# Two row groups of the TensorE array for h and for the transposes of u, in an attention and feed-forward kernel

## The chip, the cores and the metric

The kernel runs on one core of a Trainium2 chip. The metric is the device time of one execution in microseconds (us). Times of single instructions come from one execution that was recorded with the hardware profiler; they are given in us, or in ns where that is said.

## The reference

Two stages, one behind the other, over 4 batches of 12608 tokens with 128 channels; 49 agents per batch; `d_ff` is 1024. All data is float32.

```python
def sm(a, b):
    s = scale * (a @ b.transpose(0, 2, 1))
    s = s - s.max(-1, keepdims=True)
    e = np.exp(s)
    return e / (e.sum(-1, keepdims=True) + 1e-09)
a2k = sm(agents, k)
agent_v = a2k @ v
q2a = sm(q, agents)
x = (q2a @ agent_v).reshape(B * S, D)

h = x @ w_in
e = np.exp(h - h_max)
solu = h * (e / (e.sum(-1) + 1e-09))
ln = (solu - mu) / np.sqrt(var + 1e-06) * g_ln
out = ln @ w_out
```

## The kernel before, in words

**Tiles.** A tile x is 128 tokens; there are 99 per batch and 396 in all. Everything after the attention is done tile by tile, the softmax of q against the agents in units of 8 tiles and groups of 4, the second matmul w in pairs of tiles, and the output in groups of 4.

**Phase A, once per batch** (`phase_a`): the agents' softmax over the keys and its product with v, in 13 chunks of up to 1024 keys: scores (`p1_mm`, L427), maximum, exp, four transposes (`p2_t`, L460), the product with v (`p2_mm`, L476). Then `agent_v` is multiplied by `w_in` and split into a high and a low fp32r part, `mh` and `ml`, of 1024 columns each (`f3`, `f4h`, `f4l`). The 64 rows of the 49 agents (padded with zeros) stand twice, in partitions 0 to 63 and 64 to 127. Phase A of batch 0 is the head of the kernel; that of each later batch is woven into the tiles of the batch before.

**Phase B, once per 8 tiles** (`phase_b`): scores of q against the agents (`b0`, L657), softmax on DVE and ACT, and for each group of 4 tiles the division into `pack` on POOL (`b4`), two transposes (`b5`, L692), the high part of p on ACT (`b6`, L698), the low part on DVE (`b7`, L703), and DMAs that bring them into `pT` (`b8`, L716).

**Per tile.** h (`c_h`, L757, PE) into one of two PSUM buffers `ph` of two banks each; its maximum (`c_max`, L761, DVE); exp (`c_exp`, L771, ACT); u = h * e / 1024 (`c_u`, L776, DVE); the sum of squares (`c_sq`, L782, ACT); eight 128x128 transposes of u (`c_t`, L789, PE), four to a PSUM bank `px`; each bank copied out (`c_ev`, ACT) either straight into the high part `uH` (L804, then `c_ldir`, L813, subtracts on DVE for the low part `uL`) or into `uT` (L808), from which POOL makes `uH` (`c_sph`, L817) and `uL` (`c_spl`, L821). 5 of 16 banks go the first way. w (`c_w`, L837, PE) is 24 matmuls of 256 columns for a pair of tiles: three products (wH·uH, wH·uL, wL·uH) of eight pieces. The output is scaled with the tokens' factors (`c_rstd`, nine small POOL instructions per four tiles, and `c_fin`, L902, DVE) and stored.

**How h is made of parts.** p = pH + pL stands as 128 rows: 64 of pH and 64 of pL. One matmul of `pT` (128 rows) with `mh` therefore gives (pH + pL)·mh, and a second one with `ml` adds (pH + pL)·ml. With 1024 columns in two halves these are four matmuls of 512 columns per tile.

**Modes of the array.** `p1_mm`, `p2_mm` and `b0` use 64 of the 128 columns each, two at a time, one in each column half (128*64 in the profile); all other matmuls of the kernel before use the whole array (128*128).

**What sets the order.** `Plan` (L26) is a list scheduler that runs when the program is built. Each operation has an engine, a cost, a due time (`at(x, ...)` with the constants `DH` to `DEVL`), dependencies, and may take a PSUM bank (`take`) out of four `px` banks, which another operation gives back (`free`). The plan simulates the engines with its own costs, picks for each engine what can start first, and among those the one due first; the program then has that order on every engine. An operation has a `kind`: 2 for the matmuls in column halves, 0 or 1 for the rest of PE; `SWITCH` is what the plan charges for going from one kind to another, and `HOLD` how much later an operation of the same kind may start and still be preferred. DMAs are all issued by SP, in the plan's order. PE, ACT, DVE, POOL and SP run their own lists in order and wait for each other through semaphores.

Of the kernel before, what the change touches and what calls it, by code (L numbers as in the profile page):

```python
# [25 lines left out]
class Plan:  # L26
# [8 lines left out]
    SWITCH = ((0.0, 0.0, 0.09), (0.0, 0.0, 0.09), (0.15, 0.12, 0.0))  # L35

    HOLD = 0.12
# [28 lines left out]
    def run(self, idle=None):  # L66
        while True:
            best = None
            for e, ops in self.cand.items():
                if not ops:  # L70
                    continue
                free = [b[0] for b in self.banks if b[0] is not None]
                first = min(free) if free else None
                at, opts, low = self.at[e], [], None
                for o in ops:
                    s = max(at, o.ready[e])
                    if o.take:
                        if first is None:
                            continue
                        s = max(s, first)  # L80
# [12 lines left out]
            if best is None:  # L93
                break
            s, e, o = best
            for z in o.eng:
                self.cand[z].remove(o)
            if o.take:
                can = [b for b in self.banks if b[0] is not None and b[0] <= s]
                bank = max(can, key=lambda b: b[0])  # L100
                bank[0], o.bank = None, bank
            if idle is not None and e == "P":
                idle(s - self.at[e])
            o.start, o.by = s, e
            if e == "S":
                hold, size, lag = o.cost
                self.at[e] = s + hold
                if size:
                    self.dma = max(self.dma, s + 2.0) + size / 0.36
                    o.end = self.dma + 0.3  # L110
                else:
                    o.end = s + lag
            else:
                c = o.cost[o.eng.index(e)] if len(o.eng) > 1 else o.cost
                if e == "P":
                    c += self.SWITCH[self.kind][o.kind]
# [16 lines left out]
def kernel(  # L133
# [11 lines left out]
    nc = tc.nc  # L145
# [28 lines left out]
    DMX = 10.86
    DEX = 3.43
    DU_ = -4.09
    DSQ = 18.85
    DT = -0.42
    DEV = 5.18
# [33 lines left out]
    DWL = 1.6  # L213
# [4 lines left out]
    AEND = -1.6  # L218
# [425 lines left out]
    def phase_b(k, dues, gate=()):  # L644
# [50 lines left out]
        def b6(q):  # L695
            w = (min(GT, nt - q * GT) + 1) // 2 * P
            r["n", q] = bpool.tile([P, 2, GT // 2 * P], F32R, tag="pn", bufs=2, name=f"pn{b}_{t0}_{q}")
            nc.scalar.copy(out=r["n", q][:, 0, :w], in_=r["pt", q][:, :w])  # L698
# [35 lines left out]
        for q in range(nq):  # L734
# [5 lines left out]
            B5[k, q] = op("P", lambda px, q=q: b5(q, px), 0.218, dues[5] + 2.5 * q, [B4[k, q]], take=True, shy=shy)  # L740
            a6 = op("A", lambda q=q: b6(q), 0.25, dues[5] + 2.5 * q + 0.3, [B5[k, q], pT_op[groups[g - 2]] if g > 1 else None], shy=shy)
            d7 = op("D", lambda q=q: b7(q), 0.33, dues[5] + 2.5 * q + 0.6, [a6], free=B5[k, q], shy=shy)
            pT_op[groups[g]] = op("S", lambda q=q: b8(q), (0.24, 0.13 if k else 0, 3.0), dues[5] + 2.5 * q + 0.6,
                                  [d7, grp_h.get(groups[g - PTB]) if g >= PTB else None], shy=shy)
# [5 lines left out]
    def c_h(x, hf):  # L750
# [3 lines left out]
        lhs = pTs[b, g][:, j * P : (j + 1) * P]  # L754
        sl = slice(hf * HW, (hf + 1) * HW)
        for m in range(2):
            nc.tensor.matmul(ph[:, sl], lhs, bmats[b]["mh" if m == 0 else "ml"][:, sl], start=(m == 0), stop=(m == 1))  # L757
# [27 lines left out]
    def c_t(x, hf, pt):  # L785
        rr[x, hf] = pt
        for kf in range(4):
            k0 = hf * 4 + kf
            nc.tensor.transpose(pt[:, kf * P : (kf + 1) * P], us[x][0][:, k0 * P : (k0 + 1) * P], ident)  # L789
# [4 lines left out]
    def parts(x, k0, k1):  # L794
# [3 lines left out]
        return [t[:, k0:k1, j * P : (j + 1) * P] for t in pr[i]]  # L798

    def c_ev(x, hf):  # L800
        uH, _ = parts(x, hf * 4, hf * 4 + 4)
        pt = rr[x, hf].rearrange("p (k t) -> p k t", t=P)
        if direct(x, hf):
            nc.scalar.copy(out=uH, in_=pt)  # L804
        else:
            if x not in rr:
                rr[x] = epool.tile([P, NF, P], F32, tag="uT", bufs=UTB, name=f"uT{x}")
            nc.scalar.copy(out=rr[x][:, hf * 4 : hf * 4 + 4, :], in_=pt)  # L808

    def c_ldir(x, hf):  # L810
        uH, uL = parts(x, hf * 4, hf * 4 + 4)
        pt = rr[x, hf].rearrange("p (k t) -> p k t", t=P)
        nc.vector.tensor_tensor(out=uL, in0=pt, in1=uH.bitcast(F32), op=ALU.subtract)  # L813

    def c_sph(x, k0, k1):
        uH, _ = parts(x, k0, k1)
        nc.gpsimd.tensor_scalar(out=uH, in0=rr[x][:, k0:k1, :], scalar1=1.0, scalar2=0.0, op0=ALU.mult, op1=ALU.add)  # L817

    def c_spl(x, k0, k1):
        uH, uL = parts(x, k0, k1)  # L820
        nc.gpsimd.tensor_tensor(out=uL, in0=rr[x][:, k0:k1, :], in1=uH.bitcast(F32), op=ALU.subtract)  # L821
# [136 lines left out]
    for x in range(n):  # L958
# [11 lines left out]
        grp_h[b, t // GT] = last_h[b] = H[x, 1]  # L970
        MX[x] = op("D", F(c_max, x), 1.13, at(x, DMX, DMXR, DMXL), [H[x, 0], H[x, 1]])
# [5 lines left out]
        if len(dh) < 2:  # L977
# [3 lines left out]
            if len(utl) <= UTB:  # L981
                buf += wready if (len(utl) + 2) % UTB == 2 else cout
        for hf in range(2):
            T[x, hf] = op("P", F(c_t, x, hf), 0.435, at(x, DT, DTR, DTL) + 0.02 * hf, [U[x]] + buf, take=True)
            EV[x, hf] = op("A", F(c_ev, x, hf), 0.477, at(x, DEV, DEVR, DEVL) + 0.02 * hf, [T[x, hf]],
                           free=None if hf in dh else T[x, hf])
            if hf in dh:
                LD[x, hf] = op("D", F(c_ldir, x, hf), 0.602, at(x, DLD, DLDR, DLDL), [EV[x, hf]], free=T[x, hf])
        need = [[LD.get((x, hf)), EV[x, hf]] for hf in range(2)]
        if len(dh) < 2:  # L990
            k0, k1 = (4 if 0 in dh else 0), (4 if 1 in dh else NF)
            SH[x] = op("G", F(c_sph, x, k0, k1), 0.17 + 0.107 * (k1 - k0), at(x, DSP, DSPR, DSPL),
                       [EV[x, hf] for hf in range(2) if hf not in dh])
            SP[x] = op("G", F(c_spl, x, k0, k1), 0.16 + 0.268 * (k1 - k0), at(x, DSP, DSPR, DSPL) + 0.02, [SH[x]])
# [6 lines left out]
        if x % 2 == 1:  # L1001
            prev = None
            for m0 in range(0, WM, WC):
# [4 lines left out]
                       need_prev[0] + (need_prev[1] if m1 > WM // 2 else []) + wready + [prev, W.get((i - 1, 1)), FIN.get(G - 2)], take=lead, kind=0)  # L1008
# [79 lines left out]
```

## Time and profile before

| | |
|---|---|
| median of 3 runs | 1539.29 us (1538.47 to 1539.41) |
| profiled execution | 1537.99 us, span 1535.9 us |
| granted TensorE clock | 0.998 |
| matmuls | 12643 |
| DMA | 159.65 MB, mean 104 GB/s |

The span runs from the first to the last instruction of the profiled execution. In the views, `out<-in` are the tiles that an instruction writes and reads; `xN` counts instructions; the mean duration of one is in ns. In the groups of instructions the last field is the idle time of the engine before them and what ended it. In the list of waits stand the waiting engine with its instruction, what it waited for, the total in us, how often, and the longest. PE is TensorE's matmuls, PEld its weight loads, DVE VectorE, ACT ScalarE, POOL GpSimd, SP the engine that issues DMAs. A float32 matmul that isn't a transpose is recorded as two.

### The profile page before, as it was taken

The page shows a single profiled execution, that of the slowest core. Times are in us where ns is not written, and L with a number is a line of the kernel's source. Part 1 is how long each engine was busy: PE and PEld are TensorE (multiplying, and loading weights), DVE is VectorE, ACT ScalarE, POOL GpSimd, SP SyncE. Part 2 cuts the span into 40 slices and gives each one's busy share as a digit, 9 for nine tenths or more (in the row PEclk, how much of TensorE's full clock was granted, in tenths as well). Part 3 has the DMA queues.
Part 4 walks back from the last instruction along what each step waited for, and adds up shares of the span by engine and source line. Part 5 has one row for each costly group of instructions (what it writes and reads, how often), then busy time and mean ns, then how long its engine had stood idle before and what let it go on. Part 6 is the DMA issues. An engine that isn't in the chain of part 4 may idle for free.

```text
span 1535.9 us, 35549 instructions
## 1 busy us (share of the span) xinstructions
PE 1509.6 (98%) x12643; PEld 1352.4 (88%) x12643; DVE 1366.4 (89%) x2201; ACT 1424.4 (93%) x2747; POOL 1251.6 (81%) x1613
## 2 busy tenths in 40 slices
PE   8899999999999999999999999999999999999998
PEld 5688898898888898989898998989998999999988
DVE  7788998898989988988999988889999989999896
ACT  4699999999999999899999999999999999999997
POOL 2469878888887888778877798888888898998987
PEclk9999999999999999999999999999999999999999
DMA  9632423332324332423234332433222323231211
GB/s 371 190 128 73 146 91 111 96 101 94 95 77 151 111 111 90 139 82 104 82 97 136 106 118 87 128 99 104 68 89 61 87 66 90 72 86 56 63 56 46
DMA packets 114720, 159.65 MB, mean 104 GB/s; under 512 B 16240, under 2 KB 71152, under 8 KB 114544
## 3 DMA queue, kind: packets, MB, share of 16 engines
q1 hardware_dynamic: 114544, 157.39, 33.0%
q8 instruction: 100, 1.64, 0.4%
q14 instruction: 76, 0.62, 0.1%
HBM read 105.36 MB, written 26.02 MB: 86 GB/s over the span
## 4 chain that ended last, share of the span: by engine, by line
PE 73%; ACT 9%; POOL 7%; DVE 5%; issue 4%; DMA 2%; DVEq 0%; SPq 0%; ACTq 0%; POOLq 0%
PE px L837 28%; PE ph L757 18%; PE px L789 17%; ACT e L771 4%; POOL uL L821 3%; PE px L476 2%; PE px L427 2%; PE px L657 2%; ACT sq L782 2%; POOL uH L817 2%; ACT uT L808 2%; DVE u L776 1%; PE px L460 1%; PE px L692 1%; POOL y L856 1%
## 5 line engine op out<-in xcount | busy, mean ns | idle before, releaser
L821 POOL TENSOR_TENSOR uL<-uT,uH 128x1024 fp32r<-128x1024 f32 (+1 forms) x344 | 661.9, 1924 | 25.3
L761 DVE TENSOR_REDUCE nm<-ph 128x1 f32<-128x1024 f32 x396 | 479.2, 1215 | 73.9 <-PE ph L757 72.5
L776 DVE SCALAR_TENSOR_TENSOR u<-ph,e 128x1024 f32<-128x1024 f32 x396 | 480.4, 1218 | 41.9 <-ACT e L771 31.1
L782 ACT ACTIVATE sq<-u,su 128x1024 bf16<-128x1024 f32 x396 | 463.7, 1171 | 23.0 <-DVE u L776 19.7
L771 ACT ACTIVATE e<-ph,nm 128x1024 f32<-128x1024 f32 x396 | 449.0, 1137 | 16.9 <-DVE nm L761 15.3
L837 PE MATMUL px<-uL,wH 128*128 128x256 f32 x1584 | 461.6, 291 | 1.3 <-POOL uL L821 1.3
L837 PE MATMUL px<-uH,wH 128*128 128x256 f32 x1584 | 451.9, 285 | 4.2 <-DVE uL L813 2.0
L837 PE MATMUL px<-uH,wL 128*128 128x256 f32 x1584 | 448.8, 283 | 0.0
L789 PE MATMUL px<-ident,u 128*128 128x128 f32 x3168 | 430.1, 273 | 2.8 <-DVE u L776 1.6
L789 PEld LDWEIGHTS px<-ident,u 128*128 128x128 f32 x3168 | 365.2, 141 | 40.1 <-DVE ob L902 2.5
L757 PE MATMUL ph<-mh,pT 128*128 128x512 f32 x792 | 334.3, 422 | 5.2 <-DMA pT<-pn 2.4
L817 POOL TENSOR_SCALAR uH<-uT 128x1024 fp32r<-128x1024 f32 (+1 forms) x344 | 298.5, 868 | 46.8 <-ACT uT L808 44.7
L837 PEld LDWEIGHTS px<-uH,wH 128*128 128x128 f32 x1584 | 298.8, 189 | 19.4 <-issue 5.7
L808 ACT COPY uT<-px 128x512 f32<-128x512 f32 x541 | 301.6, 592 | 13.0 <-PE px L789 4.8
L757 PE MATMUL ph<-ml,pT 128*128 128x512 f32 x792 | 313.0, 395 | 0.1
L837 PEld LDWEIGHTS px<-uL,wH 128*128 128x128 f32 x1584 | 298.9, 189 | 7.9 <-issue 3.0
L837 PEld LDWEIGHTS px<-uH,wL 128*128 128x128 f32 x1584 | 299.0, 189 | 5.5 <-issue 1.4
L813 DVE TENSOR_TENSOR uL<-px,uH 128x512 fp32r<-128x512 f32 x251 | 167.9, 683 | 9.9 <-ACT uH L804 9.2
L757 PEld LDWEIGHTS ph<-mh,pT 128*128 128x128 f32 x792 | 149.6, 189 | 30.6 <-issue 6.8
L757 PEld LDWEIGHTS ph<-ml,pT 128*128 128x128 f32 x792 | 150.2, 190 | 16.5 <-DVE ml L552 0.6
L804 ACT CAST uH<-px 128x512 fp32r<-128x512 f32 x251 | 147.2, 606 | 2.4 <-PE px L789 2.0
L856 POOL TENSOR_TENSOR y<-x,nhalf 128x4 f32<-128x4 f32 x99 | 100.1, 1011 | 7.7
(118 smaller groups left out, 1344.8 us busy)
## 6 DMA issues: line engine op xcount, KB each, us to landing
pT<-pn SPq DMA_DIRECT2D x392, 64.0 KB
rB<-dr SPq DMA_DIRECT2D x98, 256.0 KB
qt<-in_qT_dram SPq DMA_DIRECT2D x48, 512.0 KB
out_dram<-ob SPq DMA_DIRECT2D x95, 256.0 KB
kt<-in_kT_dram SPq DMA_DIRECT2D x36, 512.0 KB
vt<-in_v_dram SPq DMA_DIRECT2D x36, 512.0 KB
dr<-yr SPq DMA_DIRECT2D x392, 0.5 KB
kh<-in_kT_dram SPq DMA_DIRECT2D x12, 512.0 KB
```

The source lines that it names most:

```text
L757: nc.tensor.matmul(ph[:, sl], lhs, bmats[b]["mh" if m == 0 else "ml"][:, sl], start=(m == 0), stop=(m == 1))
L761: nc.vector.tensor_reduce(out=nms[x], in_=phs[x], op=ALU.max, axis=AX.X, negate=True)
L771: nc.scalar.activation(out=es[x], in_=phs[x], func=AF.Exp, bias=nms.pop(x), accum_out=st[G]["S"][:, j : j + 1])
L776: nc.vector.scalar_tensor_tensor(out=u, in0=phs[x], scalar=INV, in1=es[x], op0=ALU.mult, op1=ALU.mult, accum_out=su)
L782: nc.scalar.activation(out=sq, in_=u, func=AF.Square, bias=su, scale=-float(DF), accum_out=st[G]["Q"][:, j : j + 1])
L789: nc.tensor.transpose(pt[:, kf * P : (kf + 1) * P], us[x][0][:, k0 * P : (k0 + 1) * P], ident)
L804: nc.scalar.copy(out=uH, in_=pt)
L808: nc.scalar.copy(out=rr[x][:, hf * 4 : hf * 4 + 4, :], in_=pt)
L813: nc.vector.tensor_tensor(out=uL, in0=pt, in1=uH.bitcast(F32), op=ALU.subtract)
L817: nc.gpsimd.tensor_scalar(out=uH, in0=rr[x][:, k0:k1, :], scalar1=1.0, scalar2=0.0, op0=ALU.mult, op1=ALU.add)
L821: nc.gpsimd.tensor_tensor(out=uL, in0=rr[x][:, k0:k1, :], in1=uH.bitcast(F32), op=ALU.subtract)
L837: nc.tensor.matmul(po, wt[:, kf, :], ut[:, kf, :], start=(q == 0), stop=(q == WM - 1))
```

## The change

- **h** is three products instead of two of doubled rows: pH·mh, pH·ml and pL·mh (pL·ml is left out). Each has 64 rows. The columns 0 to 511 are computed by rows 0 to 63 of the array, 512 to 1023 by rows 64 to 127, into the two banks of `ph`; the two matmuls of a pair follow one another. Six matmuls per tile instead of four.
- **p** is no longer stacked. `pT` has two planes: plane 0 is what ACT and DVE write (high and low part, each with the even tiles of the group in rows 0 to 63 and the odd ones in 64 to 127), plane 1 the same with the row halves exchanged, brought by two DMAs per group instead of four. There are four such tiles instead of eight of half the size.
- **The transposes of u** take 64 tokens each: sixteen instead of eight per tile, with 128 columns of weights and 64 moving columns, the tokens 0 to 63 in rows 0 to 63 and the others in rows 64 to 127, alternating. The two token halves go to two banks, which are both taken when the transposes start (`take=2`).
- **The copies** of a tile's transposes therefore divide by tokens instead of by pieces of `d_ff`: 8 rows of 64 instead of 4 rows of 128 per bank; the same holds for POOL's and DVE's half tiles. Every w matmul now needs both halves.
- **The plan** has a kind 3 for both, which `SWITCH` charges for going in and out, `HOLD` is 0.49 instead of 0.12 and holds for kind 3 too, and the due times are other numbers. Which 5 of 16 banks go straight to `uH` stays.

```diff
-    SWITCH = ((0.0, 0.0, 0.09), (0.0, 0.0, 0.09), (0.15, 0.12, 0.0))
-    HOLD = 0.12
+    SWITCH = ((0.0, 0.0, 0.09, 0.15), (0.0, 0.0, 0.09, 0.15), (0.15, 0.12, 0.0, 0.15), (0.19, 0.19, 0.15, 0.03))
+    HOLD = 0.49
...
-                if e == "P" and self.kind == 2:
-                    near = [z for z in opts if z[0] <= low + self.HOLD and z[1].kind == 2] or near
+                if e == "P" and self.kind >= 2:
+                    near = [z for z in opts if z[0] <= low + self.HOLD and z[1].kind == self.kind] or near
...
-    DH = -3.24
+    DH = -5.61
...
-    PTB = 8
+    PTB = 4
...
-            r["n", q] = bpool.tile([P, 2, GT // 2 * P], F32R, tag="pn", bufs=2, name=f"pn{b}_{t0}_{q}")
-            nc.scalar.copy(out=r["n", q][:, 0, :w], in_=r["pt", q][:, :w])
+            pT = pTs[b, t0 // GT + q] = bpool.tile([P, 2, 2, GT // 2 * P], F32R, tag="pT", bufs=PTB, name=f"pT{b}_{t0}_{q}")
+            nc.scalar.copy(out=pT[:, 0, 0, :w], in_=r["pt", q][:, :w])
...
             for i in range(2):
-                w = (m + 1 - i) // 2
-                r0 = i * AP2
-                for part in range(2):
-                    r1 = r0 if part == 0 else AP2 - r0
-                    nc.sync.dma_start(out=to[r1 : r1 + AP2, :w, i, :].bitcast(F32),
-                                      in_=pn[r0 : r0 + AP2, part, : w * P].rearrange("a (g p) -> a g p", p=P).bitcast(F32))
+                r0, r1 = i * AP2, (1 - i) * AP2
+                nc.sync.dma_start(out=pT[r1 : r1 + AP2, 1, :, :w].bitcast(F32), in_=pT[r0 : r0 + AP2, 0, :, :w].bitcast(F32))
...
-    def c_h(x, hf):
+    def c_h(x):
...
-        sl = slice(hf * HW, (hf + 1) * HW)
-        for m in range(2):
-            nc.tensor.matmul(ph[:, sl], lhs, bmats[b]["mh" if m == 0 else "ml"][:, sl], start=(m == 0), stop=(m == 1))
+        mh, ml = (bmats[b][m] for m in ("mh", "ml"))
+        tok = slice(j // 2 * P, j // 2 * P + P)
+        for q, (part, mm) in enumerate(((0, mh), (0, ml), (1, mh))):
+            for hf in range(2):
+                sl, rows = slice(hf * HW, (hf + 1) * HW), slice(hf * AP2, (hf + 1) * AP2)
+                nc.tensor.matmul(ph[:, sl], pTs[b, g][rows, (hf + j) % 2, part, tok], mm[rows, sl], start=(q == 0), stop=(q == 2))
...
-    def c_t(x, hf, pt):
-        rr[x, hf] = pt
-        for kf in range(4):
-            k0 = hf * 4 + kf
-            nc.tensor.transpose(pt[:, kf * P : (kf + 1) * P], us[x][0][:, k0 * P : (k0 + 1) * P], ident)
+    def c_t(x, *pts):
+        u = us[x][0]
+        for th in range(2):
+            rr[x, th] = pts[th]
+        for k in range(NF):
+            for th in range(2):
+                rows = slice(th * AP2, (th + 1) * AP2)
+                nc.tensor.transpose(pts[th][:, k * AP2 : (k + 1) * AP2], u[rows, k * P : (k + 1) * P], ident[rows, rows])
...
-        for hf in range(2):
-            H[x, hf] = op("P", F(c_h, x, hf), 0.468, at(x, DH, DHR, DHL) + 0.02 * hf,
-                          [pT_op[b, t // GT], U.get(x - 2)] + mdone[b][: hf + 1], kind=0)
+        H[x] = op("P", F(c_h, x), 0.70, at(x, DH, DHR, DHL), [pT_op[b, t // GT], U.get(x - 2)] + mdone[b], kind=3)
...
+        T[x, 0] = T[x, 1] = op("P", F(c_t, x), TCOST, at(x, DT, DTR, DTL), [U[x]] + buf, take=2, kind=3)
         for hf in range(2):
-            T[x, hf] = op("P", F(c_t, x, hf), 0.435, at(x, DT, DTR, DTL) + 0.02 * hf, [U[x]] + buf, take=True)
```

The changed kernel's lines stand one or two away from those before: h is L755, the transposes L790, w L839, the copies into `uT` L810 and into `uH` L806, the DMAs of `pT` L713.

On SP, in the third batch, the DMAs of one group's `pT` and of the scale factors (`dr`, `rB`) before:

```order
L716 DMA pT_96_0_11398<-pn_96_0_11371 64x2x128
L716 DMA pT_96_0_11398<-pn_96_0_11371 64x128
L716 DMA pT_96_0_11398<-pn_96_0_11371 64x2x128
L716 DMA pT_96_0_11398<-pn_96_0_11371 64x128
L878 DMA dr_11438<-yr_11431 4x32 x4
L918 DMA out_dram<-ob_11465 128x512
L879 DMA rB_11439<-dr_11438 128x512
```

and after:

```order
L880 DMA dr_12982<-yr_12974 4x32 x4
L713 DMA pT_96_0_13006<-pT_96_0_13006 64x512 x2
L881 DMA rB_12983<-dr_12982 128x512
L920 DMA out_dram<-ob_13129 128x512
```

The group's DMAs are two, and stand between the write and the broadcast of the scale factors. The places on PE are shown in the prediction.

More of the change, by code (lines that the diff above doesn't have):

```diff
@@ L71, in run @@
                     continue
-                free = [b[0] for b in self.banks if b[0] is not None]
-                first = min(free) if free else None
+                free = sorted(b[0] for b in self.banks if b[0] is not None)
                 at, opts, low = self.at[e], [], None
@@ L77, in run @@
                     if o.take:
-                        if first is None:
+                        if len(free) < o.take:
                             continue
-                        s = max(s, first)
+                        s = max(s, free[o.take - 1])
                     opts.append((s, o))
@@ L99, in run @@
                 can = [b for b in self.banks if b[0] is not None and b[0] <= s]
-                bank = max(can, key=lambda b: b[0])
-                bank[0], o.bank = None, bank
+                o.bank = sorted(can, key=lambda b: -b[0])[: int(o.take)]
+                for b in o.bank:
+                    b[0] = None
             if idle is not None and e == "P":
@@ L119, in run @@
             if o.free is not None:
-                o.free.bank[0] = o.end + self.LAT[e + "P"]
+                of, i = o.free if isinstance(o.free, tuple) else (o.free, 0)
+                of.bank[i][0] = o.end + self.LAT[e + "P"]
             if o.fn:
-                args = [o.bank[1]] if o.take else []
+                args = [b[1] for b in o.bank] if o.take else []
                 if len(o.eng) > 1:
@@ L163 @@
     UB = 8
+    TCOST = 0.496
     TD = 2
     WC = 4
-    BD0 = 11.76
-    BD1 = 15.6
+    BD0 = 13.83
+    BD1 = 17.06
     BD2 = 30.39
-    BD3 = -27.34
-    BD4 = -2.08
-    BD5 = 4.61
-    DH = -3.24
[L174 to L179, printed above, removed]
+    BD3 = -28.93
+    BD4 = -7.3
+    BD5 = 5.96
+    DH = -5.61
+    DMX = 14.19
+    DEX = 1.81
+    DU_ = 16.45
+    DSQ = 23.46
+    DT = -3.69
+    DEV = 3.44
     DLD = 0.41
-    DSP = 17.32
-    DW = 3.32
+    DSP = 16.59
+    DW = 3.39
     DR = 14.7
-    DF_ = 14.05
+    DF_ = 14.12
     OUTD = -4.87
@@ L191 @@
     VLAG = 5.87
-    PTB = 8
+    PTB = 4
     SHY = -0.0
     DHR = -4.39
-    DHL = -5.43
-    DMXR = 17.18
+    DHL = -6.08
+    DMXR = 8.74
     DMXL = 5.41
     DEXR = 23.76
-    DEXL = -1.81
+    DEXL = -4.24
     DUR = -10.07
@@ L204 @@
     DTR = -6.53
-    DTL = -23.89
-    DEVR = -14.39
+    DTL = -24.6
+    DEVR = -8.6
     DEVL = 9.51
     DLDR = -16.1
-    DLDL = 26.96
+    DLDL = 21.86
     DSPR = -6.87
@@ L739, in phase_b @@
             B4[k, q] = op("G", lambda q=q: b4(q), 0.08 + 0.53 * sc, dues[4] + 2.5 * q, [d5, old])
[L740 to L741 removed]
+            B5[k, q] = op("P", lambda px, q=q: b5(q, px), 0.218, dues[5] + 2.5 * q,
+                          [B4[k, q], grp_h.get(groups[g - PTB]) if g >= PTB else None], take=True, shy=shy)
+            a6 = op("A", lambda q=q: b6(q), 0.25, dues[5] + 2.5 * q + 0.3, [B5[k, q]], shy=shy)
             d7 = op("D", lambda q=q: b7(q), 0.33, dues[5] + 2.5 * q + 0.6, [a6], free=B5[k, q], shy=shy)
[L743 to L744 removed]
+            pT_op[groups[g]] = op("S", lambda q=q: b8(q), (0.12, 0.13 if k else 0, 2.5), dues[5] + 2.5 * q + 0.6, [d7], shy=shy)
         if k + 2 < nu and k + 2 > 1:
@@ L797, in parts, with c_ev @@
             pr[i] = [gpool.tile([P, NF, 2 * P], F32R, tag=t, name=f"{t}{x}") for t in ("uH", "uL")]
[L798 to L803, printed above, removed]
+        o = j * P + t0 * AP2
+        return [t[:, :, o : o + (t1 - t0) * AP2] for t in pr[i]]
+    def c_ev(x, th):
+        uH, _ = parts(x, th, th + 1)
+        pt = rr[x, th].rearrange("p (k t) -> p k t", t=AP2)
+        if direct(x, th):
             nc.scalar.copy(out=uH, in_=pt)
@@ L807, in c_ev, with c_ldir, c_sph, c_spl @@
                 rr[x] = epool.tile([P, NF, P], F32, tag="uT", bufs=UTB, name=f"uT{x}")
[L808 to L812, printed above, removed]
+            nc.scalar.copy(out=rr[x][:, :, th * AP2 : (th + 1) * AP2], in_=pt)
+    def c_ldir(x, th):
+        uH, uL = parts(x, th, th + 1)
+        pt = rr[x, th].rearrange("p (k t) -> p k t", t=AP2)
         nc.vector.tensor_tensor(out=uL, in0=pt, in1=uH.bitcast(F32), op=ALU.subtract)
[L815 to L821, printed above, removed]
+    def c_sph(x, t0, t1):
+        uH, _ = parts(x, t0, t1)
+        nc.gpsimd.tensor_scalar(out=uH, in0=rr[x][:, :, t0 * AP2 : t1 * AP2], scalar1=1.0, scalar2=0.0, op0=ALU.mult, op1=ALU.add)
+    def c_spl(x, t0, t1):
+        uH, uL = parts(x, t0, t1)
+        nc.gpsimd.tensor_tensor(out=uL, in0=rr[x][:, :, t0 * AP2 : t1 * AP2], in1=uH.bitcast(F32), op=ALU.subtract)
     WM = 3 * NF
@@ L1007 @@
                 o = op("P", f, 0.1192 * (m1 - m0), at(x, DW, DWR, DWL) + 2.0 * m0 / WM,
-                       need_prev[0] + (need_prev[1] if m1 > WM // 2 else []) + wready + [prev, W.get((i - 1, 1)), FIN.get(G - 2)], take=lead, kind=0)
+                       need_prev[0] + need_prev[1] + wready + [prev, W.get((i - 1, 1)), FIN.get(G - 2)], take=lead, kind=0)
                 if lead:
```

32 lines of the change are left out of this document (15 added, 17 removed).

## The prediction

> **What bounds the kernel now.** I read the page first: its span and the busy time of each engine.
>
> ```profile
> span 1535.9 us, 35549 instructions
> PE 1509.6 (98%) x12643; PEld 1352.4 (88%) x12643; DVE 1366.4 (89%) x2201; ACT 1424.4 (93%) x2747; POOL 1251.6 (81%) x1613
> ```
>
> PE is the fullest, but ACT is close, and a share of the span mixes stages. So next I read the busy times by stretch; the cuts are at the head (before the first h) and about where each batch of 99 tiles ends.
>
> ```profile
> 60.00:435.00 375.00, 365.49 (x3046) 327.09 (x3045) 335.32 (x535) 351.76 (x675) 300.15 (x385) 1.00 0.33 103
> 435.00:809.00 374.00, 370.46 (x3132) 335.12 (x3131) 337.56 (x544) 353.88 (x684) 310.06 (x399) 1.00 0.34 105
> 809.00:1182.00 373.00, 372.69 (x3153) 338.46 (x3151) 335.71 (x539) 355.01 (x688) 310.20 (x401) 1.00 0.33 100
> 1182.00:1519.00 337.00, 334.38 (x2728) 305.99 (x2728) 307.59 (x473) 330.53 (x623) 303.15 (x386) 1.00 0.25 71
> sum 1476.00, PE 1454.98 PEld 1317.50 DVE 1323.91 ACT 1396.96 POOL 1230.56; mean PE 291.00 PEld 263.50 DVE 264.78 ACT 279.39 POOL 246.11
> ```
>
> The columns after the length are PE, PEld, DVE, ACT, POOL. The first three batches, which carry the next batch's phase A, take 374 us each with PE busy nearly all of it; the fourth has no phase A and takes 337 us, and there PE (334) and ACT (331) are both full. The sum runs to the end: PE is busy 1455 of 1476 us after the head, 98.6%. The list of waits agrees: the longest waits of the others are for PE, or for each other; none of PE's own comes near them.
>
> ```profile
> DVE nm L761 <- PE ph L757: 72.5, 117, 2.4
> PE ph L757 <- DMA pT<-pn: 2.4, 2, 1.5
> ```
>
> **The change part by part, on PE.** What h, the transposes and w cost is the distance between starts in the timeline (the second column is a duration, which overlaps the next one).
>
> ```profile
> 800.81 0.40 PE L757 MATMUL ph<-mh,pT 128*128 128x512 f32 x1
> 801.74 0.28 PE L837 MATMUL px<-uH,wL 128*128 128x256 f32 x1
> ...
> 808.41 1.03 PE L789 MATMUL px<-ident,u 128*128 128x128 f32 x8
> 809.20 0.36 PE L837 MATMUL px<-uH,wL 128*128 128x256 f32 x1
> 809.40 0.28 PE L837 MATMUL px<-uH,wH 128*128 128x256 f32 x1
> ```
>
> Four h matmuls lie between 800.81 and 801.74: 0.93 us, 0.235 each. Eight transposes and one w matmul lie between 808.41 and 809.40; a w matmul comes every 0.12 us (366.01 to 366.13 below), so the transposes take 0.87, 0.109 each.
>
> The trace has no matmul in row groups. Its nearest are the matmuls in column groups, L476 and L657, which stand in pairs too:
>
> ```profile
> 366.01 0.28 PE L837 MATMUL px<-uL,wH 128*128 128x256 f32 x1
> 366.13 0.28 PE L837 MATMUL px<-uH,wL 128*128 128x256 f32 x1
> 366.34 1.09 PE L476 MATMUL px<-vt,eT 128*64 128x128 f32 x16
> 367.36 0.38 PE L837 MATMUL px<-uH,wH 128*128 128x256 f32 x1
> 367.58 0.28 PE L837 MATMUL px<-uL,wH 128*128 128x256 f32 x1
> ...
> 399.61 0.40 PE L757 MATMUL ph<-ml,pT 128*128 128x512 f32 x1
> 399.94 2.07 PE L657 MATMUL px<-ag_sb,qt 128*64 128x49 f32 x64
> 401.94 0.33 PE L789 MATMUL px<-ident,u 128*128 128x128 f32 x1
> ```
>
> Three things are read here. First, pairs overlap: 64 matmuls of L657 take 2.00 us, 0.031 each, and 16 of L476 about 0.055 each, half of the 0.109 of a full-array matmul that streams the same 128 f32 columns. Second, changing the array's mode costs: from 366.13 to 367.58 are 1.45 us, less two w (0.24) and 8 pairs of L476 at 0.109 (0.87), so 0.34 for going in and out, 0.17 a change. Third, a first weight load that nothing hides shows in the duration: 0.38 against 0.28 for w (0.10), and 0.33 against the 0.27 of the mean below for a transpose (0.06).
>
> ```profile
> L789 PE MATMUL px<-ident,u 128*128 128x128 f32 x3168 | 430.1, 273 | 2.8 <-DVE u L776 1.6
> ```
>
> h becomes three pairs of 512 columns. If a pair runs as one, 3 x 0.24 = 0.72; saved 0.22 a tile, 87 us in 396. Ends: 0.235 a pair (two at once) and 0.47 (one after the other); I take 0.24, because the column pairs do overlap.
>
> The transposes become eight pairs of 64 moving columns, each member with a load of 128 columns. Half of 0.109 is 0.054, L657's pair takes 0.058 with loads of 64 columns (2.00 less 0.14 of the mode change, over 32), and the load by itself is 0.06. I take 0.06: 8 x 0.06 = 0.48; saved 0.39, 154 us. Ends: 0.054 and today's 0.109.
>
> The mode changes are counted in PE's order: 154 before, 879 after, since nearly every tile has its own block of row-group work (393 blocks). 725 more at 0.175 (0.17, and the load that opens a block is a transpose's 0.06 or an h's 0.10 where L476's was about 0.05) are +127 us. Ends: 0.09 (66 us) and 0.20 (145 us).
>
> PE's sum: 1455 - 87 - 154 + 127 = **1341 us**, 114 less.
>
> **What is next: ACT.** The change gives ACT no work to save. Its time per tile, from start to start:
>
> ```profile
> 815.70 1.15 ACT L782 ACTIVATE sq<-u,su 128x1024 bf16<-128x1024 f32 x1 [0.23 <-DVE u L776]
> ...
> 816.85 1.05 ACT L808 COPY uT<-px 128x512 f32<-128x512 f32 x2
> 817.79 1.12 ACT L771 ACTIVATE e<-ph,nm 128x1024 f32<-128x1024 f32 x1
> ...
> 818.89 0.59 ACT L808 COPY uT<-px 128x512 f32<-128x512 f32 x1
> 819.35 0.61 ACT L804 CAST uH<-px 128x512 fp32r<-128x512 f32 x1
> ```
>
> sq 1.15, two copies 0.94, exp 1.10: 3.19 a tile, 1263 us in 396. The small groups add about 85 after the head:
>
> ```profile
> L698 ACT CAST pn<-px 128x256 fp32r<-128x256 f32 x100 | 38.7, 387 | 2.1 <-PE px L692 2.0
> L453 ACT ACTIVATE ek<-px,nmp 128x512 f32<-128x512 f32 x48 | 33.0, 688 | 15.9 <-DVE nmp L439 15.5 <-PE ph L757 0.2
> L673 ACT ACTIVATE logits<-logits 128x392 f32<-128x392 f32 x48 | 25.3, 529 | 7.8 <-DVE logits L669 7.3
> L466 ACT COPY eT<-px 128x512 f32<-128x512 f32 x34 | 20.3, 596 | 8.4 <-PE px L460 8.4
> L444 ACT ACTIVATE fc<-nmp 128x1 f32<-128x1 f32 x48 | 14.2, 297 | 0.0
> ```
>
> (131.5 in all; a quarter of the 67.5 of L453, L466 and L444 lies in the head; and a row overlaps the next by about 0.13, as the copy of 0.59 above that is followed after 0.46, which is 32 us in some 245 instructions: 83.) So ACT is occupied for about 1350 us after the head: far below PE's 1455 today, but above PE's 1341 afterwards. ACT ends last, by little. Its copies now write rows of 64 (128x8x64) instead of 128. L673, in rows of 49, takes 529 ns where the line from 256 columns (387) to 512 (596) gives 498: 0 to 0.03 a copy, 0 to 24 us. I take 0; rows of 128 into uH cost no more than the contiguous ones (the copies stand about 0.47 apart either way).
>
> POOL keeps its instructions with rows of 64; busy 1231, and 303 of 337 in the fourth batch, so below ACT unless it is slower by a tenth. DVE, 1324 busy, keeps its own.
>
> **What moves in the order.** PE, in the third batch, around one tile (px are the four free PSUM banks, ph the two h buffers, pack the source of pT), before:
>
> ```order
> L837 MATMUL px_126<-uH_10191,wH 128x256
> L692 MATMUL px_124<-ident,pack_110 128x128 x2
> L757 MATMUL ph_123<-mh_5767,pT_72_1_10228 128x512
> L757 MATMUL ph_123<-ml_5768,pT_72_1_10228 128x512
> L757 MATMUL ph_123<-mh_5767,pT_72_1_10228 128x512
> L757 MATMUL ph_123<-ml_5768,pT_72_1_10228 128x512
> L789 MATMUL px_127<-ident,u_10429 128x128 x4
> L789 MATMUL px_125<-ident,u_10429 128x128 x4
> L837 MATMUL px_126<-uL_10192,wH 128x256
> ```
>
> and after, the end of one block of row-group work:
>
> ```order
> L790 MATMUL px_126<-ident,u_12506 128x64
> L790 MATMUL px_124<-ident,u_12506 128x64
> L755 MATMUL ph_123<-mh_6444,pT_80_1_12023 128x512 x2
> L755 MATMUL ph_123<-ml_6445,pT_80_1_12023 128x512 x2
> L755 MATMUL ph_123<-mh_6444,pT_80_1_12023 128x512 x2
> L839 MATMUL px_127<-uL_12343,wH 128x256
> ```
>
> One transpose of a tile and one h, in either order, share a block, so a tile pays for one way in and one way out. A transpose now needs both its banks free before it starts: PE stands behind the later of two copies where it stood behind one, and w is queued behind it.
>
> On SP a group's pT was four DMAs and is two, of the same bytes in all; PE's waits for them were 2.4 us, so I cost it at nothing. pT's first half is now written by ACT and DVE directly, into one of four buffers instead of eight, so ACT's write waits for the DMA and the h of four groups (16 tiles) ago, long done; without that distance it would stop ACT's queue.
>
> **The sum.** The head stays, 60 us. After it two engines have 1341 and 1350 us of work. PE alone at the limit kept 98.6%; in the fourth batch, the nearest case of two full engines, ACT's 3.19 a tile and 0.11 for L698 and L673 (64.0, less 148 x 0.13, over 396) are over 98 tiles 323 of 337 us, 96%. 1350 / 0.96 = 1406; 60 + 1406 = 1466 span. The profiled execution took 1537.99 for a span of 1535.9, 2.1 more, and lies 1.3 under the median 1539.29: **1469 us**, 4.6% less.
>
> **The rivals.**
>
> *Loads pace the transposes (slower).* If a load of 128 columns in a row group takes as long as one of w, 0.10 to 0.11, each pair waits for its loads, at 0.109: the transposes save nothing, PE has 1455 - 87 + 127 = 1495, /0.986 = 1516, 1579 us. It decides from 0.096 a pair, where 8 x (0.109 - 0.096) x 396 = 40 no longer pays the 127 less the 87. Against it: a transpose's load that nothing hides showed 0.06. The Trainium skill, "TensorE: Matmul & The Clock Gate", section "LDWEIGHTS (loading the stationary operand)", gives columns / 1.2 ns however few rows are loaded, an estimate of 107 ns for each of these; w's 0.10 agrees with it, the transposes' 0.06 doesn't. 0.08.
>
> *Pairs overlap only in part.* A pair of h that takes a third longer than one matmul (0.31, a third of the way from 0.235 to 0.47) costs 3 x 0.07 x 396 = 83 more, PE 1424, /0.986 = 1444, 1507 us: faster still, but PE remains the bound. L476's pairs, at twice 0.055, show no such loss, which speaks against it. The Trainium skill, "TensorE: Matmul & The Clock Gate", section "Part 3: Packing small matmuls", gives 3.07 times for four row groups; by that ratio, as an estimate, 0.235 / 0.77 = 0.31. With this case goes PE held up by the two banks: 0.1 us a tile is 40 us, 1509. 0.17.
>
> *Row groups don't run side by side at all.* h 6 x 0.235 = 1.41, +186 us; transposes 16 x 0.06, +36; changes +127: 1804 / 0.986 = 1830, 1893 us. 0.03.
>
> *Both engines run as full as PE did.* 1350 / 0.986 = 1369, 1433 us. 0.07.
>
> **How the numbers follow.** The forecast has 0.65. The range goes from the last rival, 1433, to past the second with the copies' bound of 0.03 (12 of 24 us), 1520; outside are the two slower cases, 0.11, and about half of the 0.07 and of the tail above: 0.17. About 0.2%, 3 us, is what a measurement of this kernel can tell from no change. Faster 0.87; slower 0.11; between the two, 0.02, if a pair lands at 0.096.
>
> **What would show it.** Right: L755 pairs 0.24 apart, eight L790 pairs in 0.48, 0.17 a mode change, PE busy about 1340 to 1400, ACT above 96% of each batch. Wrong: pairs at 0.11 or h at 0.47; ACT's copies above 0.5 start to start; PE waiting for ACT's copies (banks) by more than 40 us; the fourth batch not under 337 us.

## The result, and the profile after

| | before | after |
|---|---|---|
| median | 1539.35 us | 1514.11 us |
| ratio | | 0.9838, 95% interval 0.9821 to 0.9855 |
| span of the profiled execution | 1535.9 us | 1512.5 us |

The changed kernel is 1.6% faster. The forecast was 1469 us, 4.6%: the direction is right, the size is off by a factor of nearly three. One execution of the experiment with h alone took 2990.62 us where its three others took 1594.92 to 1597.61, and its median below is that of the three.

The page's line of busy times, after:

```profile
PE 1438.1 (95%) x16609; PEld 1169.1 (77%) x16609; DVE 1369.3 (91%) x2211; ACT 1408.6 (93%) x2737; POOL 1253.6 (83%) x1613
```

PE isn't full any more, and no other engine is. PE's busy time counts a duration that overlaps the next one, so what was saved is better read from starts. The timeline of PE, one block of row-group work in the third batch:

```profile
804.45 0.71 PE L790 MATMUL px<-ident,u 64*128 64x64 f32 x16
804.97 0.48 PE L755 MATMUL ph<-mh,pT 64*128 64x512 f32 x2
805.28 0.39 PE L755 MATMUL ph<-ml,pT 64*128 64x512 f32 x2
805.52 0.40 PE L755 MATMUL ph<-mh,pT 64*128 64x512 f32 x2
805.84 0.39 PE L839 MATMUL px<-uH,wH 128*128 128x256 f32 x1
806.06 0.31 PE L839 MATMUL px<-uL,wH 128*128 128x256 f32 x1
```

Sixteen transposes take 0.52 us, of which about 0.06 is the first load: 0.06 a pair. The first pair of h takes 0.31, as the first h matmul behind transposes did before (803.47 to 803.78); the second and third stand 0.24 apart. From the third pair at 805.52 to w at 805.84 are 0.32, 0.24 for the pair and 0.08 to 0.09 for the change of mode, and w's second matmul comes 0.22 later instead of 0.12, the load of 0.10 that nothing hides. Each PE term of the sum came out near its forecast.

The stretches of the batches after, cut at the first maximum of each (the columns are length, PE, PEld, DVE, ACT, POOL):

```profile
62.00:423.00 361.00, 344.73 (x4056) 280.86 (x4054) 332.73 (x539) 344.30 (x669) 299.22 (x383) 0.99 0.35 107
423.00:785.00 362.00, 349.65 (x4079) 285.82 (x4077) 334.87 (x541) 349.46 (x681) 307.49 (x395) 1.00 0.36 109
785.00:1155.00 370.00, 357.11 (x4200) 292.16 (x4196) 340.24 (x552) 351.32 (x684) 312.32 (x401) 1.00 0.34 103
1155.00:1489.00 334.00, 313.94 (x3650) 261.36 (x3649) 306.77 (x469) 327.39 (x622) 304.26 (x391) 0.99 0.24 70
1489.00:1512.50 23.50, 15.63 (x136) 13.55 (x134) 10.56 (x15) 8.12 (x16) 8.48 (x13) 0.84 0.09 29
```

By the same mark (first maxima at 60.1, 433.0, 808.8 and 1178.9 us, the last at 1519.1) the batches before took 373, 376, 370 and 340 us. So the first two gained 12 and 14 us, the third nothing, and the fourth, which had two full engines already, 6. The end after the last maximum is 23.5 us, 6.5 longer than the 17 before. Most of PE's saving didn't arrive in the time. The list of waits shows where it went; first before:

```profile
POOL x L853 <- ACT sq L782: 73.6, 68, 4.3
...
POOL uH L817 <- ACT uT L808: 44.7, 33, 10.4
DVE u L776 <- ACT e L771: 31.1, 88, 1.3
...
PEld px L837 <- issue: 10.1, 23, 0.8
...
PEld px L837 <- POOL uL L821: 3.3, 6, 1.5
...
PEld ph L757 <- DVE u L776: 2.4, 5, 0.8
```

and after:

```profile
POOL x L855 <- ACT sq L780: 72.4, 48, 6.5
PEld px L839 <- issue: 48.7, 132, 0.8
DVE u L774 <- ACT e L769: 41.0, 89, 2.0
PEld ph L755 <- DVE u L774: 36.2, 81, 1.0
POOL uH L819 <- ACT uT L810: 31.7, 24, 8.7
DVE nm L759 <- PE ph L755: 29.8, 57, 2.5
PEld px L839 <- POOL uL L823: 18.8, 28, 3.4
```

DVE's wait for h fell from 72.5 to 29.8, and POOL's waits for ACT, which were there before, fell a little. What grew is DVE's wait for ACT (31.1 to 41.0) and, above all, the waits of PE's weight loads: for DVE to read h out of its buffer (2.4 to 36.2), for POOL (3.3 to 18.8), and for nothing that the profile shows (10.1 to 48.7, for the loads of w). The chain that ended last, as shares of the span, says the same; first before:

```profile
PE 73%; ACT 9%; POOL 7%; DVE 5%; issue 4%; DMA 2%; DVEq 0%; SPq 0%; ACTq 0%; POOLq 0%
```

and after:

```profile
PE 41%; ACT 25%; DVE 21%; issue 9%; POOL 3%; DMA 1%; ACTq 0%; DVEq 0%; SPq 0%; POOLq 0%
```

Before, one engine carried the end; after, the chain runs through three.

### The profile page after: what moved, and what is told of

It is laid out like the page before. It is cut to its first block, busy times and chain, and to the rows that moved or that the text cites. A ratio compares the mean times of both kernels' runs of the same rounds, so it can differ in the third digit from the quotient of the medians.

```text
span 1512.5 us, 43191 instructions
## 1 busy us (share of the span) xinstructions
PE 1438.1 (95%) x16609; PEld 1169.1 (77%) x16609; DVE 1369.3 (91%) x2211; ACT 1408.6 (93%) x2737; POOL 1253.6 (83%) x1613
## 4 chain that ended last, share of the span: by engine, by line
PE 41%; ACT 25%; DVE 21%; issue 9%; POOL 3%; DMA 1%; ACTq 0%; DVEq 0%; SPq 0%; POOLq 0%
PE px L839 18%; PE ph L755 9%; ACT e L769 8%; ACT sq L780 7%; PE px L790 6%; DVE u L774 6%; ACT uT L810 6%; DVE nm L759 6%; DVE uL L815 3%; PE px L478 2%; ACT uH L806 2%; PE px L429 2%; POOL uL L823 2%; PE px L659 1%; DVE ob L904 1%
## 5 line engine op out<-in xcount | busy, mean ns | idle before, releaser
L759 DVE TENSOR_REDUCE nm<-ph 128x1 f32<-128x1024 f32 x396 | 477.2, 1214 | 30.8 <-PE ph L755 29.8
L780 ACT ACTIVATE sq<-u,su 128x1024 bf16<-128x1024 f32 x396 | 470.9, 1189 | 16.5 <-DVE u L774 14.4
L839 PE MATMUL px<-uH,wH 128*128 128x256 f32 x1584 | 463.5, 293 | 14.9 <-ACT uT L810 9.3
L839 PE MATMUL px<-uL,wH 128*128 128x256 f32 x1584 | 454.4, 287 | 8.6 <-POOL uL L823 8.4
L839 PE MATMUL px<-uH,wL 128*128 128x256 f32 x1584 | 455.6, 288 | 0.0
L755 PE MATMUL ph<-mh,pT 64*128 64x512 f32 x1584 | 350.0, 441 | 15.7 <-DVE u L774 13.1
L839 PEld LDWEIGHTS px<-uH,wH 128*128 128x128 f32 x1584 | 299.4, 189 | 52.6 <-issue 23.9
L839 PEld LDWEIGHTS px<-uL,wH 128*128 128x128 f32 x1584 | 299.3, 189 | 29.2 <-issue 13.5
L810 ACT COPY uT<-px 128x512 f32<-128x512 f32 x541 | 308.2, 614 | 13.3 <-issue 6.7
L839 PEld LDWEIGHTS px<-uH,wL 128*128 128x128 f32 x1584 | 299.1, 189 | 16.2 <-issue 11.4
L790 PEld LDWEIGHTS px<-ident,u 64*128 64x128 f32 x6336 | 240.5, 139 | 78.3 <-ACT uT L810 14.0
L790 PE MATMUL px<-ident,u 64*128 64x64 f32 x6336 | 272.4, 226 | 12.0 <-DVE uL L815 3.1
L755 PEld LDWEIGHTS ph<-mh,pT 64*128 64x128 f32 x1584 | 150.7, 186 | 88.7 <-DVE u L774 36.2
L755 PE MATMUL ph<-ml,pT 64*128 64x512 f32 x792 | 158.4, 394 | 0.1
L806 ACT CAST uH<-px 128x512 fp32r<-128x512 f32 x251 | 151.8, 625 | 1.8 <-PE px L790 1.8
L769 ACT ACTIVATION_READ_ACCUMULATOR e<-ph,nm 128x1 f32 x396 | 93.2, 235 | 0.0
```

Source lines behind the costliest of these rows:

```text
L755: nc.tensor.matmul(ph[:, sl], pTs[b, g][rows, (hf + j) % 2, part, tok], mm[rows, sl], start=(q == 0), stop=(q == 2))
L759: nc.vector.tensor_reduce(out=nms[x], in_=phs[x], op=ALU.max, axis=AX.X, negate=True)
L769: nc.scalar.activation(out=es[x], in_=phs[x], func=AF.Exp, bias=nms.pop(x), accum_out=st[G]["S"][:, j : j + 1])
L780: nc.scalar.activation(out=sq, in_=u, func=AF.Square, bias=su, scale=-float(DF), accum_out=st[G]["Q"][:, j : j + 1])
L790: nc.tensor.transpose(pts[th][:, k * AP2 : (k + 1) * AP2], u[rows, k * P : (k + 1) * P], ident[rows, rows])
L810: nc.scalar.copy(out=rr[x][:, :, th * AP2 : (th + 1) * AP2], in_=pt)
```

## The experiments

The question was what holds the time now: PE still (theory P), ACT (A), POOL (Q), the ring of h, maximum, exp and u through the two h buffers (R), waits that the row groups bring (B), or no engine alone, because four lists in a fixed order wait for each other in turn (S). Each run's median stands beside the kernel before on the same chip (medians of 1539.8 to 1540.6 us in the four sets, so a comparison across sets is good to about a microsecond) or beside the changed kernel's 1514.

### Half of sq: less for ACT, outside the ring

```diff
-        nc.scalar.activation(out=sq, in_=u, func=AF.Square, bias=su, scale=-float(DF),
+        nc.scalar.activation(out=sq[:, :HW], in_=u[:, :HW], func=AF.Square, bias=su, scale=-float(DF),
```

> The changed kernel with its order kept; the sum of squares reads 512 of the 1024 columns (half of it is left out), so ACT has about 0.43 us a tile less, 170 us in all; sq lies outside the ring h, maximum, exp, u, next h. If ACT alone is the bound (theory A): 1450 to 1475, where PE's 1341 us of work take over at 96%. If the ring through the two h buffers with its queueing is the bound (theory R): 1495 or more, at most 20 off. If PE is still the bound through mode changes and its own waits (theory P): 1508 to 1520.

Measured: 1484.98 us, ratio to before 0.9645 (0.9621 to 0.9668), 29 less than the changed kernel. None of the three bands: ACT matters more than R and P say, but of 170 us taken out of it 29 arrive.

### Half of exp: less for ACT, inside the ring

```diff
-        nc.scalar.activation(out=es[x], in_=phs[x], func=AF.Exp, bias=nms.pop(x), accum_out=st[G]["S"][:, j : j + 1])
+        nc.scalar.activation(out=es[x][:, :HW], in_=phs[x][:, :HW], func=AF.Exp, bias=nms.pop(x), accum_out=st[G]["S"][:, j : j + 1])
...
-        nc.vector.scalar_tensor_tensor(out=u, in0=phs[x], scalar=INV, in1=es[x], op0=ALU.mult, op1=ALU.mult, accum_out=su)
+        nc.vector.scalar_tensor_tensor(out=u.rearrange("p (h f) -> p h f", h=2), in0=phs[x].rearrange("p (h f) -> p h f", h=2), scalar=INV,
+                                       in1=es[x][:, :HW].unsqueeze(1).to_broadcast([P, 2, HW]), op0=ALU.mult, op1=ALU.mult, accum_out=su)
```

> The changed kernel with its order kept; exp is computed for 512 of the 1024 columns and u uses those twice (half of exp is left out). ACT is relieved by the same 170 us as with the halved sq, but inside the ring. A: the same as with the halved sq, 1450 to 1475. R: clearly less than with the halved sq, by 25 or more, 1440 to 1465. P: 1508 to 1520.

Measured: 1482.97, 0.9627 (0.9606 to 0.9648). The same as with the halved sq within 2 us, as A says, though not in A's band. That the cut lies in the ring makes no difference: R falls.

### One of w's three products left out: less for PE

```diff
-            mm += [(wH, uH, kf), (wH, uL, kf), (wL, uH, kf)]
+            mm += [(wH, uH, kf), (wH, uL, kf), None]
```

> The changed kernel with its order kept; w leaves out the product of uH with the low part of w, 16 matmuls a pair of tiles instead of 24: PE has 187 us less. P: 1430 to 1460, ACT's 1350 at 96 to 98%. A: 1500 to 1515. R: 1495 to 1515, since w is outside the ring and delays it only where an h is queued behind it.

Measured: 1504.51, 0.9764 (0.9743 to 0.9784); 10 less for 187 us of PE's work. P falls; the time lies in the bands of A and of R. The waits of this run show what takes PE's place:

```profile
PEld ph L755 <- DVE u L774: 109.0, 191, 1.9
...
PE ph L755 <- DVE u L774: 62.1, 129, 1.7
```

PE, done early, stands before h until u has left the buffer: its wait for DVE rises from 36 and 13 us to 109 and 62.

### Half of the maximum: less for DVE

```diff
-        nc.vector.tensor_reduce(out=nms[x], in_=phs[x], op=ALU.max, axis=AX.X, negate=True)
+        nc.vector.tensor_reduce(out=nms[x], in_=phs[x][:, :HW], op=ALU.max, axis=AX.X, negate=True)
```

> The changed kernel with its order kept; the maximum reads 512 of the 1024 columns (half of it is left out): DVE has about 0.5 us a tile less, inside the ring. R: 1450 to 1480. A and P: 1505 to 1518, as DVE is neither's bound.

Measured: 1501.32, 0.9747 (0.9727 to 0.9767); 13 less for about 200 us. Below the band of A and P, and far above that of R. DVE now waits 116.6 us for exp where it waited 41.0:

```profile
DVE u L774 <- ACT e L769: 116.6, 167, 2.5
```

### Half of POOL's subtraction

```diff
-        nc.gpsimd.tensor_tensor(out=uL, in0=rr[x][:, :, t0 * AP2 : t1 * AP2], in1=uH.bitcast(F32), op=ALU.subtract)
+        nc.gpsimd.tensor_tensor(out=uL[:, :4], in0=rr[x][:, :4, t0 * AP2 : t1 * AP2], in1=uH[:, :4].bitcast(F32), op=ALU.subtract)
...
-            mm += [(wH, uH, kf), (wH, uL, kf), (wL, uH, kf)]
+            mm += [(wH, uH, kf), (wH, uL, kf % 4), (wL, uH, kf)]
```

> The changed kernel with its order kept; POOL makes the low part of u for four of the eight pieces only, and w uses those twice (half of that subtraction is left out). POOL has about 1.1 us less for a whole tile and 0.6 for a half, some 300 us of its 1330 (start to start, 3.36 a tile). If POOL, counted start to start, is the hidden bound (theory Q): 1430 to 1470. If no engine alone holds the time and the lists wait for each other in turn (theory S): 1485 to 1508, as the three others gave 10 to 31 us each.

Measured: 1509.23, 0.9808 (0.9792 to 0.9825); 5 less, though POOL's busy time fell by 298, and one above S's band:

```profile
PE 1431.7 (95%) x16609; PEld 1166.2 (77%) x16609; DVE 1365.8 (91%) x2211; ACT 1407.7 (93%) x2737; POOL 955.4 (63%) x1613
```

Q falls: POOL's lateness in the trace comes from what it waits for.

### All four cuts at once

The edits for sq, the maximum, w and POOL together (w with `(wH, uL, kf % 4)` and without the third product).

> The changed kernel with its order kept and four cuts at once: half of sq (ACT, 170 us), half of the maximum (DVE, 200 us), one of three products of w (PE, 187 us), half of POOL's subtraction (300 us); each left out as in the single runs. S: the engines wait for each other's full lists, so all cuts together give far more than the sum of the single ones (83 us with POOL's taken as 30): 1300 to 1380. If the ring h, maximum, exp, u through the two h buffers holds the time by its latency (theory R; only the maximum in it is cut, 0.5 us a tile or 0.25 in a ring of two tiles): 1400 to 1440, little more than the sum.

Measured: 1366.99, 0.8881 (0.8867 to 0.8895); 147 less than the changed kernel, where the four singly gave 29 + 13 + 10 + 5 = 57. That is what S says: what one list gains is lost at the next as long as that one stays full. A bound that passes from engine to engine would say it too. And again no engine is full:

```profile
PE 1266.3 (93%) x15025; PEld 984.8 (72%) x15025; DVE 1164.1 (85%) x2211; ACT 1242.2 (91%) x2737; POOL 953.1 (70%) x1613
```

### HOLD at 0.12 and at 0.9

```diff
-    HOLD = 0.49
+    HOLD = 0.12
```

> The changed kernel with HOLD at 0.12 as before: PE's order has 1054 changes of mode instead of 879, 175 more at 0.175, 31 us of work for PE. Theory P (PE's mode changes hold the time): 1540 to 1550. S: the waits take part of it, 1518 to 1540. If the long HOLD costs PE waiting for work of the same mode (theory H): 1490 to 1510.

Measured: 1546.02, 1.0041 (1.0018 to 1.0065); 32 more, as P said and beyond S's band, and for 175 more changes of mode 0.18 us each. Taken alone that fits the price of a change.

```diff
-    HOLD = 0.49
+    HOLD = 0.9
```

> The changed kernel with HOLD at 0.9: 764 changes of mode instead of 879, 20 us less work for PE, and PE may be kept up to 0.9 us for work of the same mode. If each change of mode is paid in full, as the step from 0.12 to 0.49 suggested (175 changes, 32 us): 1490 to 1498. If waiting for work of the same mode takes it back: 1508 to 1535.

Measured: 1545.73, 1.0037 (1.0025 to 1.0049). With 115 changes fewer the kernel is 32 slower as well, beyond both bands. So the agreement of the run before is no proof of P: both numbers give another order, and both other orders cost the same.

### The changed kernel with the due times of before

```diff
-    DH = -5.61
+    DH = -3.24
...
-    DU_ = 16.45
+    DU_ = -4.09
```

(and the other due times of the diff; `HOLD` and `PTB` stay).

> The changed kernel with the due times of the kernel before (HOLD stays 0.49; 896 changes of mode, 17 more, 3 us): the same work on every engine in another order. If the order holds the time (theory S): 1530 to 1600. If the engines' work or their latencies hold it whatever the order: 1512 to 1522.

Measured: 1541.83, 1.0016 (1.0006 to 1.0026). The same work on every engine but for 17 changes of mode more, and all of the gain is gone. With these due times the row groups are worth nothing.

### Each part alone

With the due times of before: h alone (the hunks of `c_h`, `b6` to `b8`, `PTB` and `Plan`), then the transposes alone (`c_t`, `parts`, the copies and `Plan`).

```diff
-        for hf in range(2):
-            H[x, hf] = op("P", F(c_h, x, hf), 0.468, ...
+        H[x] = op("P", F(c_h, x), 0.70, ..., kind=3)
```

> The kernel before with h alone in row groups (p unsplit, its new DMAs and buffers, HOLD 0.49), the transposes as before, the due times as before; to be set beside the run with both parts and the same due times (1541.8). PE's order has 806 changes of mode, 652 more than before: 114 us at 0.175, against 87 saved: 27 more for PE. If the change of mode is paid by either part alone (theory M): 1560 to 1580. If h alone is worth its 87 and the transposes bring only waits: 1490 to 1520.

Measured: 1595.06, 1.0365 (1.0344 to 1.0385); 55 more than before. Most of that is work of PE, which is as full as in the kernel before and 45 us longer busy:

```profile
PE 1554.6 (98%) x13444; PEld 1285.0 (81%) x13444; DVE 1372.8 (86%) x2201; ACT 1428.7 (90%) x2747; POOL 1253.3 (79%) x1613
```

```diff
+        T[x, 0] = T[x, 1] = op("P", F(c_t, x), TCOST, at(x, DT, DTR, DTL), [U[x]] + buf, take=2, kind=3)
         for hf in range(2):
-            T[x, hf] = op("P", F(c_t, x, hf), 0.435, ..., take=True)
```

> The kernel before with the transposes alone in row groups (two banks at once, copies by tokens, HOLD 0.49), h and p as before, the due times as before. 900 changes of mode, 746 more: 131 us, against 147 saved (eight pairs at 0.0625 for 0.87): 16 less for PE. M: 1525 to 1550. If the transposes' need of two banks at once costs by itself (theory B): 1555 or more.

Measured: 1591.35, 1.0332 (1.0316 to 1.0347). Alone each part is over 3% slower, both together 0.2% with the same due times. A tile pays for about one way into row groups and one out whether one or two parts use it; that is theory M, in direction. In size both lie 15 us or more beyond M's bands. For h the forecast of 27 more for PE was too low: its page shows 45. For the transposes PE was forecast 16 less, and the page has it busy for 1520.5 us, 11 more than before, at 96% of the span; the rest of the 51 is time in which PE waits. The transposes' figure is the one that B named. But the order was not searched for either, and this doesn't part B from a poor order.

### Work taken from PE and ACT, in both kernels

The two edits, one product of w and half of sq, together in the changed kernel:

> The changed kernel with its order kept and two cuts at once: half of sq (ACT, 170 us) and one of three products of w (PE, 187 us), both left out. Singly they gave 29 and 10. If cuts add (no coupling): 1470 to 1480. S: with both relieved, DVE's and POOL's 1330 are what is left, at the 93% that the changed kernel reaches 1430 plus the head of 60 is an upper end; 1440 to 1465.

Measured: 1458.66, 0.9471 (0.9451 to 0.9491); 55 less, singly 29 and 10.

The same cuts in the kernel before, which has no row group: w, then sq, then both.

> The kernel before with its order kept and one of the three products of w left out: PE has 187 us less (1455 to 1268), without a row group in the program. If any relief of PE ends at the other engines (theory S): 1490 to 1520, though the cut is larger than the change's 114. If the row groups' own waits cost the changed kernel its gain (theory B): 1440 to 1475.

Measured: 1519.52, 0.9856 (0.9839 to 0.9872).

> The kernel before with its order kept and half of sq left out: ACT has 170 us less. PE has 1455 us of 1476 there, so S and B both: 1525 to 1540; the same cut gave 29 in the changed kernel.

Measured: 1533.22, 0.9952 (0.9938 to 0.9967).

> The kernel before with its order kept and both cuts, one product of w and half of sq. S: both together give far more than the two singly, as in the changed kernel (55 against 39): 1440 to 1475. B: 1420 to 1440.

Measured: 1453.82, 0.9440 (0.9426 to 0.9454).

Theory B falls here as the main cause, and each of S's bands is met. In the kernel before, 187 us less for PE give 21, without any row group; the change, an estimated 114 less, gave 25. 170 less for ACT give 7, as ACT wasn't the bound; both together 87, three times the sum. B's 1440 to 1475 for the first isn't met. The busy times of the first of these, w cut in the kernel before:

```profile
PE 1415.6 (93%) x11059; PEld 1176.3 (77%) x11059; DVE 1360.0 (90%) x2201; ACT 1419.9 (93%) x2747; POOL 1252.0 (82%) x1613
```

ACT at 93%, PE at 93%: the changed kernel's picture, made without its change. And its chain:

```profile
ACT 34%; DVE 24%; PE 19%; issue 16%; DMA 4%; POOL 2%; SPq 0%; ACTq 0%; DVEq 0%; POOLq 0%
```

Beside it the kernel before with only sq cut, where PE remains alone:

```profile
PE 91%; DVE 4%; DMA 3%; issue 1%; ACT 1%; POOL 1%; SPq 0%; DVEq 0%; ACTq 0%; POOLq 0%
```

One reading these runs don't part from S is a bound that simply passes to the next fullest engine. By the pages the fullest engine is busy for 93 to 96% of the span in every run with a cut, except where only sq is cut in the kernel before (99%): PE for 96% in the changed kernel with half of sq, ACT for 94% with w cut there, DVE for 93% with both, PE for 93% with all four. That alone makes two cuts together bring more than their sum. What it leaves open is why the share is 93 to 96% where PE alone at the limit had 98 to 99% (the kernel before, and before with sq cut), and why another order of the same work costs 28 to 32 us.

## Why the prediction was wrong, point by point

**What bounds the kernel before.** Right: PE. The cut in ACT moved it by 0.5%.

**The price of h and of the transposes.** Right: 0.24 and 0.06 a pair as taken, but for the first pair of h (0.31). The rival that the loads pace the transposes is out: at 0.109 a pair sixteen of them would take 0.87, and they take 0.52 with the first load. The Trainium skill, "TensorE: Matmul & The Clock Gate", section "LDWEIGHTS (loading the stationary operand)", gives columns / 1.2 ns, an estimate of 107 ns for a load of 128 columns; for the transposes' loads in two row groups the measurement, a pair with its two loads every 0.06 us, decides otherwise. The rival of pairs that overlap in part is out too: two groups of 512 columns take 0.24, as one does. The ratio of 3.07 that the Trainium skill, "TensorE: Matmul & The Clock Gate", section "Part 3: Packing small matmuls", gives for four row groups doesn't carry over to two. That rival's other half, PE held up by the two banks, isn't needed either: in the changed kernel the transposes waited 16.6 us for copies into `uT` and 11.4 for `uL` (2.8 and 1.2 before), and in the kernel before with w cut, where each needs one bank, 23.6 for either.

**The price of a change of mode.** Right: 0.08 to 0.09 and the load that nothing hides, 0.10 for w, as in the column groups. No run measures PE's sum of 1341 as such. On the measure of its starting point, 1455 us of busy time, the rows above add to 1381, within the 1340 to 1400 named; part of the 40 more is the ends of durations where PE then waits (a w counts as 0.28 and takes 0.12).

**What is next.** Half right. ACT has the most work of those left, and a cut in it gives more than one in any other engine. But "ACT ends last" was read as if ACT would then run like a bound.

**The sum: the step that failed.** "1350 / 0.96 = 1406": the 96% was taken from the fourth batch as the nearest case of two full engines. That is one batch, without phase A, of another order. In the changed kernel the time after the head is 1512.5 - 62 = 1450, so ACT's 1350 are 93% of it and PE's 1341 92%: 44 us more than the sum's 1406, and with the 2 us that the head is longer the whole miss of 46 in the span. In the fourth batch itself the fullness held: ACT is busy 327.39 of 334 us there, 98%, as before (330.53 of 337). It didn't carry over to the three batches with phase A, where ACT is busy 344.30 of 361, 349.46 of 362 and 351.32 of 370, 95 to 97%; the sign "ACT above 96% of each batch" failed in two of them. The fullness was the term that decided, and the prediction took it from one row; it weighed fuller engines as a rival, and emptier ones not, though PE's 98.6% was that of an engine whose neighbours had slack. The kernel before with w cut has ACT's 1350 in the 1459 us after its head: 92.5%, the changed kernel's value by another way. Why the engines reach 93% and not 96% stays open; the runs show that it needs no row group, and that it moves with the order.

**The range.** 1514 lies inside the stated 1433 to 1520, and near the 1507 of the second rival. That is luck: the upper end stood for pairs that overlap in part and for dearer copies, and neither came about.

**The side terms.** The copies with rows of 64 cost no more, as taken. In ACT's timeline after the change two of them take 0.95 from start to start, 0.94 before:

```profile
821.89 1.05 ACT L810 COPY uT<-px 128x512 f32<-128x512 f32 x2
822.84 1.16 ACT L780 ACTIVATE sq<-u,su 128x1024 bf16<-128x1024 f32 x1
```

The end grew by 6.5 us, which the prediction had at nothing and which is part of the 44; no run isolates why, and a w that needs both halves of both tiles is only a guess. The new due times count as much as the row groups: without them the change is worth 0 of its 25 us. The prediction read the order for its changes of mode and not for what it does to the waits.

**What stays open.** Why the transposes alone are 51 us slower with the old due times, where PE's busy time grew by 11; and how much another order could still take from the 1450: besides the one on record only three were run, and each was about 30 us slower. Nor was the kernel before run with other due times, so what a search of the order alone would have given it isn't shown.

## What to carry to other kernels

Before pricing work taken from the bound, add up the work of every engine over the same stretch. If the next ones lie within a tenth, as here, most of the gain ends there: here 114 us from PE brought 25, and 187 us by another way 21. Cuts in two such engines together bring a multiple of their sum, so relieve the next engine in the same change, and search the order again, for without that this one was worth nothing. And price the time from the fullest engine that is left: in these runs it was busy for 93 to 96% of the span once others were nearly as full, and for 98 to 99% when it stood alone.

A mode of the array that costs 0.17 us a change pays only if enough work shares one block; two parts that each lose alone, as here with the old due times, can break even together, or gain once the order is searched.

## What the runs showed of the hardware

Uncertain beforehand, and now measured: two matmuls of 64 rows and 512 columns in the two row groups take 0.24 us, no more than one of 128 rows (0.235), so both stream at full rate into two PSUM banks. Transposes of 64 rows, each with a load of 128 columns, come every 0.06 us a pair. An unhidden load showed 0.06 by itself, so two of them one behind the other would need 0.12: the loads of the two groups run beside each other as well.
